# A two-layer attention and SwiGLU prompt on one core: next layer's first rounding in the middle of the last unit, layer 0's norms in two halves, the second chunk's transposes inside a product, input by two queues

## The chip, the cores and the metric

The kernel runs on one core of a Trainium2 chip. The metric is the device time of one execution in microseconds (us); for the kernel before it is the median of three runs. A profile comes from one further execution. The engines are TensorE (PE: matmuls and transposes; PEld: its weight loads), VectorE (DVE), ScalarE (ACT), GpSimd (POOL) and SyncE (SP, which here only issues DMAs). All instruction orders are written out by hand, so each engine executes its instructions in the order in which the program emits them, and waits in that order.

## The reference

The input `x` is 2048 rows of 448 floats. Two identical layers follow each other, each an attention with one key and value head for 16 query heads, and a SwiGLU feed-forward:

```python
# x: (1, 2048, 448); 16 heads of 28; wq (448, 448), wk, wv (448, 28), wo (448, 448)
def A(x):                                   # multi-query attention, no mask
    q = (x @ wq).reshape(1, 2048, 16, 28).transpose(0, 2, 1, 3)
    k, v = x @ wk, x @ wv
    p = softmax(einsum("bhqd,bkd->bhqk", q, k) * 28 ** -0.5)
    return einsum("bhqk,bkd->bhqd", p, v).transpose(0, 2, 1, 3).reshape(1, 2048, 448) @ wo
def B(x):                                   # w_gate, w_up (448, 1792); w_down (1792, 448)
    return (silu(x @ w_gate) * (x @ w_up)) @ w_down
for _ in range(2):                          # the same weights in both layers
    x = x + A(layernorm(x))                 # layernorm without gain and bias, eps 1e-5
    x = x + B(layernorm(x))
```

## The kernel before

The rows are cut into 16 tiles of 128 and four chunks (c = 0 to 3) of 512. `xres` holds all of `x` on the chip; every sum of a layer is added into it. Matmuls run on float32r operands: each operand is cut into a high part (a rounded copy, made by ScalarE or GpSimd) and a low part (value minus high part, made by VectorE or GpSimd), and a product is the sum of high times high, high times low and low times high. This cutting is called rounding below; `cut`, `flip` and `flipped` (L286 to L312) do it for a normed chunk: `xh` is the high part, `xl` the low one.

**The norm of a chunk** is made by `norm_steps` (L234). It returns a list of steps: four `stat` (two VectorE instructions each, L241 and L242, per tile of 128 rows), one `scale` (two GpSimd instructions, L246 and L247, which turn the four variances into `rstd`), and four `apply` (VectorE, L255: subtract the mean, multiply by `rstd`), each followed by a small copy on GpSimd (L257). With `away` given, the normed chunk is turned by VectorE and sent through DRAM (`send`, L265, `load`, L274); without it TensorE turns it (`flip`, L291: sixteen 128x128 transposes into four PSUM banks, four to a bank, L296), and ScalarE (`xh`, L304) and VectorE (`xl`, L309 and L312) round it from there.

**The projections** (`Attention.project`, L514) are sixteen products of 128 output columns, in the order of `self.order`: for each chunk the column blocks m = 3, 2, 0, 1. `self.seen` counts them from 0. One product (`product_T`, L318) is eleven matmuls of 128x128 by 128x512. Its result is copied out by ScalarE (L556, L558) and stored through DRAM; for m = 0 and 1 VectorE also transposes the value rows (`vt`, L565), after ScalarE's copy. Before the product whose successor (or which itself) is the first of a chunk, that chunk is flipped (`turned`); in layer 0 the flip of chunk 1 comes after product 3 instead of before it (`late`). `self.plan[n, 1]` and `self.when[n]` hold steps that are emitted after product n: there stand the norms of layer 0's chunks 1 to 3, the loads of the next chunk of `x` (`fill`), the key loads (`key_load`) and key splits (`key_split`, GpSimd).

**The scores** follow (`Attention.scores`), 256 steps per layer, and then **the feed-forward** (`FeedForward`): 14 blocks of 128 hidden columns in seven groups of two, the groups 2 to 5 by a block scheme of their own, the others as *units* (gi, c, n): group, chunk, block in the group. A unit (`unit`, L1069) is emitted in this order: eleven pairs of matmuls into two banks; `between`, one-column reads `seen` (L355) by ScalarE of both banks, which separate the two halves in which rows 0 to 63 and rows 64 to 127 write the same bank; the first of the two `down` steps of the unit before it, which ends with `between` on its four banks; ten more pairs into the same two banks; SiLU (L1110), product with the up half (L1111) and rounding of the result (`h`: L1112, `hl`: L1115), with the second `down` step among them; and then the entries of `self.soon` that are due. An entry of `soon` is a number and a function; each unit lowers the numbers of all entries in the order in which they were appended, and calls those that fall below zero. `self.mid[gi, c, n]` holds functions that a unit calls between its two halves: the first one ahead of the `down` step, the others behind it.

**The hand-over to layer 1.** In the last group (gi = 6), a chunk's last sums are added to `xres` in the first unit of the next chunk, and then `hand_over(c)` (L1035) is called: it emits the statistics and the scale of layer 1's norm of this chunk and appends what remains to `soon`. For chunk 0 that is two steps that apply, turn, send and load it; `cut` (L1053), which comes due in unit (6, 3, 0) and rounds it, four casts on ScalarE and four subtractions on VectorE; and the first three products of layer 1 (L1054), due in unit (6, 3, 1). For chunk 1 `ready` (L1044: the four applies) is appended in unit (6, 2, 0) and comes due in (6, 3, 0). After unit (6, 3, 1) follow the fourth product (with chunk 1's flip ahead of it) and `flush`, the last `down` steps.

**The start.** The four tiles of chunk 0 of `x` are loaded by SyncE (L1233), then the weights `wq`, `wk`, `wv` (`load_wqkv`) and chunk 1 (L1253). While these come, TensorE transposes the identity 54 times (L1252). The buffers that are filled with constants (`vsb`, `qraw`, `mask`, on GpSimd) come after chunk 0's norm.

Of the kernel before, what the change touches and what calls it, by code (L numbers as in the profile page):

```python
# [8 lines left out]
F32 = mybir.dt.float32  # L9
# [6 lines left out]
P = 128  # L16
# [36 lines left out]
def forward(  # L53
# [177 lines left out]
            again,  # L231
        )

    def norm_steps(c, away=None):  # L234


        got = {}
        cs = slice(4 * c, 4 * c + 4)

        def stat(t):  # L240
            nc.vector.bn_stats(stats[:, 4 * c + t, :], xres[:, 4 * c + t, :])  # L241
            nc.vector.bn_aggr(mv[:, 4 * c + t, :], stats[:, 4 * c + t, :])  # L242

        def scale():
            rstd = pers.tile([P, 4], F32, name="rstd", bufs=2)
            nc.gpsimd.tensor_scalar(rstd, mv[:, cs, 1], 1.0, EPS, ALU.mult, ALU.add)  # L246
            nc.gpsimd.tensor_tensor(rstd, rstd, halfn, ALU.pow)  # L247
            got["r"] = rstd

        def apply(t):  # L250
            if t == 0:
                got["x"] = pers.tile([P, 4, 512], F32, name="xn")
            got["o"] = (away() if away else got["x"][:, t, :])[:, 0:D]
            i, r = xres[:, 4 * c + t, :], got["r"][:, t : t + 1]
            nc.vector.tensor_scalar(got["o"], i, mv[:, 4 * c + t, 0:1], r, ALU.subtract, ALU.mult)  # L255
            if not away:
                nc.gpsimd.tensor_copy(got["x"][:, t, D:512], got["o"][:, 384:D])  # L257

        def turn(t):
            nc.vector.transpose(side()[:, :, :, t], got["o"].rearrange("p (k s) -> p k s", s=32))  # L260

        def side():
            return got["x"].rearrange("p t n -> p (t n)")[:, 0 : 4 * D].rearrange("p (k s t) -> p k s t", s=32, t=4)

        def send():  # L265
            turns.append(dram.tile([D, 512], F32, name=f"xt{len(turns)}"))
            got["xt"] = turns[-1]
            for a in range(4):
                nc.sync.dma_start(
                    got["xt"].rearrange("(k r) n -> r k n", r=32)[:, :, P * a : P * a + P],  # L270
                    side()[32 * a : 32 * a + 32].rearrange("p k s t -> p k (s t)"),
                )

        def load():  # L274
            got["raw"] = pers.tile([P, 4, 512], F32, name="xn")
            rows3(got["raw"], got["xt"])

        got["load"] = load
        fs = [lambda t=t: stat(t) for t in range(4)] + [scale]
        for t in range(4):  # L280
            fs += [lambda t=t: apply(t)] + [lambda t=t: turn(t)] * bool(away)
        return fs + [send] * bool(away), got
# [32 lines left out]

        return [(a[0][rs], b[0][rs]), (a[0][rs], b[1][rs]), (a[1][rs], b[0][rs])]

    def product_T(po, a_h, a_l, tiles, late=False):  # L318

        xh, xl = tiles[:2]  # L320
        seq, low = [], []
        for k in range(3):
            seq += [(a_h[k], xh[:, k, :]), (a_h[k], xl[:, k, :])]
            (low if late else seq).append((a_l[k], xh[:, k, :]))
        seq += low
        seq += [(a_h[3], xh[:, 3, :]), (a_l[3], xh[:, 3, :])]
        for i, (a, b) in enumerate(seq):
            nc.tensor.matmul(po, a, b, start=(i == 0), stop=(i == len(seq) - 1))  # L328

    def by_rows(upper, n, w, tiles):  # L330
# [28 lines left out]
    class Attention:  # L359
# [154 lines left out]
        def project(self):  # L514

            c, m = self.order[self.seen]
            for f in self.plan.get((self.seen, 0), ()):
                f()
            late = self.layer == 0 and self.seen == 3
            turned = [o[0] for o in self.order[self.seen : self.seen + 2] if o[1] == 3]  # L520
            for o in turned if not late else ():
                self.turned(o)
            self.q(c, m)
            for o in turned if late else ():
                self.turned(o)
            for f in self.plan.get((self.seen, 1), []) + self.when.pop(self.seen, []):
                f()
            self.seen += 1
# [2 lines left out]
            if c in self.norms:  # L531
                flip(self.norms.pop(c), self.X[c])

        def q(self, c, m):
            cs = slice(512 * c, 512 * c + 512)
            held, po = bank((3, 4, 5) if self.seen > len(self.order) - 4 else wide[-1], True)
            ms = slice(P * m, P * m + P)
            wh, wl = self.w
            product_T(po, [wh[:, k, ms] for k in range(4)], [wl[:, k, ms] for k in range(4)], self.X[c], self.layer + self.seen == 0)
            if not full and self.seen in (6, 10, 14):  # L540
                self.maxima(self.seen // 4 - 1)
            live.remove(held)
            if c not in self.qd:
                self.qd[c] = dram.tile([D, 512], F32, name=f"qd{self.layer}_{c}")
            last = self.seen == len(self.order) - 1
            raw = pers.tile([P, 512], F32, name="sg") if last else self.pool.tile([P, 512], F32, name="stage")
            if last:
                nc.scalar.copy(raw, po)
            if not full and (c or not self.layer):
                if self.seen % 2 == 0:  # L550
                    self.two = wpool.tile([P, 2, 512], F32R, tag="wgh", name="q2", bufs=FG + 1)
                self.hi[m] = self.two[0:112, self.seen % 2, :]
                if last:
                    self.rounded = lambda: nc.vector.tensor_copy(self.hi[m], raw[0:112, :])
                else:
                    nc.scalar.copy(self.hi[m], po[0:112, :])  # L556
            if not last:
                nc.scalar.copy(raw, po)  # L558
# [6 lines left out]
            nc.vector.transpose(vt, po[96:128, :])  # L565
# [217 lines left out]
    class FeedForward:  # L783
# [217 lines left out]
        def accumulate(self, gi, c, d):  # L1001
# [22 lines left out]
            def others():  # L1024
                for t in (2, 1, 3):
                    add(t)
                for t in (1, 3, 2):
                    store(t)
                live.difference_update(HIGH)
                if end and self.nxt:  # L1030
                    self.hand_over(c)

            return [begin, others]

        def hand_over(self, c):  # L1035

            a = self.nxt
            fs, got = norm_steps(c, None if c else lambda: qraw)
# [11 lines left out]
            if c == 0:  # L1050
                self.soon.append([1, lambda: [f() for f in fs[5:9]]])
                self.soon.append([2, lambda: [f() for f in (*fs[9:], got["load"], wipe)]])
                self.soon.append([4, lambda: cut(got, a.X[c])])  # L1053
                self.soon.append([5, lambda: [a.project() for _ in range(3)]])  # L1054
            elif c == 1:
                self.soon.append([2, ready])
            else:
                a.plan[4 * c - 4, 0] = [ready]

# [170 lines left out]
            self.flush()  # L1230

    for t in range(4):
        nc.sync.dma_start(xres[:, t, :], xs[:, t, :])  # L1233
    nc.gpsimd.memset(halfn, -0.5)
    nc.scalar.activation(warm, halfn[:, 0:1], AF.Exp)
    nc.gpsimd.memset(bottom, 0.0)
# [2 lines left out]
    at = Attention(0)  # L1239
    at.pool = xb.enter_context(tc.tile_pool(name="stage_", bufs=4))  # L1240
    xbp = xb.enter_context(tc.tile_pool(name="xb0", bufs=2))
    fs, got = norm_steps(0)
    for f in fs[:4]:
        f()
    parts, at.w = load_wqkv(xb.enter_context(tc.tile_pool(name="wqkv0", bufs=1)), True)
    make_identity(nc, ident)
    for f in fs[4:]:
        f()
    at.norms[0] = got
    idle = bank(LOW)[1]  # L1250
    for n in range(54):
        nc.tensor.transpose(idle[:, 0:P], ident, ident)  # L1252
    fill = lambda c: nc.sync.dma_start(xres[:, 4 * c : 4 * c + 4, :], xs[:, 4 * c : 4 * c + 4, :])  # L1253
    fill(1)
    at.below(nc.sync)
    at.X = {c: xtile(xpool if c < 2 else xbp) for c in range(NC)}
    parts[0]()
    at.turned(0)
    nc.gpsimd.memset(vsb, 0.0)
    nc.gpsimd.memset(vsb[:, :, DH : DH + 1], 1.0)  # L1260
    nc.gpsimd.memset(qraw, 0.0)
    if mask is not None:
        nc.gpsimd.memset(mask, 0.0)
        nc.gpsimd.memset(mask[:, 0:16:5, :], 1.0)
        for base, sign in ((0, 1), (DH - 1, -1)):
            nc.gpsimd.affine_select(
                out=mask, in_=mask, pattern=[[0, 16], [-DH * sign, 4]], compare_op=ALU.is_ge, fill=0.0,
                base=base, channel_multiplier=sign,
            )
    parts[1]()  # L1270
    for c in range(1, NC):
        fs, got = norm_steps(c)
        n = 4 * c - 4
        at.plan[n, 1] = [lambda c=c: fill(c + 1)] * (c < NC - 1) + fs[:5]
        at.plan[n + 1, 1] = fs[5:] + [lambda c=c, got=got: at.norms.__setitem__(c, got)]
    for layer in range(2):
        at.finish()
        xb.close()
# [33 lines left out]
```

## Time and profile before

| | before |
|---|---|
| three runs, us | 1967.7, 1967.4, 1964.23; median 1967.4 |
| the profiled execution's own time, us | 1967.23 |
| its span, first to last instruction, us | 1965.5 |
| mean granted clock of TensorE | 0.997 |
| busy: PE, PEld, DVE, ACT, POOL | 99%, 67%, 51%, 68%, 39% |
| products of layer 0 | about 12 to 63 us |
| scores of layer 0 | about 63 to 570 us |
| feed-forward of layer 0 | about 570 to 1000 us |
| layer 1 | about 1000 us to the end |

Rows of a timeline give the start, the duration, the engine, the line, the operation, output and inputs, the count where like ones were merged, and in brackets the idle time before it with what ended it. Rows of a table of windows give the stretch, its length, and the busy time (and instructions) of PE, PEld, DVE, ACT and POOL, then TensorE's granted clock (1.00 is full speed), the DMA engines' busy share and GB/s. Matmuls overlap in these rows: a dense row of them is read by the distance of the starts, not by the durations.

### The profile page before, as it was taken

How to read it: one execution, taken by the hardware profiler on the slowest of the kernel's cores; microseconds unless marked ns; L12 is line 12 of the kernel's file. 1: busy time of each engine (PE TensorE's matmuls, PEld its weight loads, DVE VectorE, ACT ScalarE, POOL GpSimd, SP SyncE). 2: the span in 40 equal slices, each digit the busy share in tenths (PEclk: the TensorE clock that was granted, in tenths of full speed). 3: DMA queues.
4: the chain of work that ended last, by engine and by line, in shares of the span. 5: the costliest groups of instructions: out<-in, count | busy, mean ns of one | idle time of the engine just before them, and what ended most of it. 6: DMA issues, size and time to landing. Idle time of an engine off the chain costs nothing. (4 is left out here: it accounts for less than half of the span.)

```text
span 1965.5 us, 45651 instructions
## 1 busy us (share of the span) xinstructions
PE 1950.6 (99%) x18315; PEld 1322.2 (67%) x18315; DVE 1012.1 (51%) x1711; ACT 1338.4 (68%) x2353; POOL 769.3 (39%) x989
## 2 busy tenths in 40 slices
PE   9999999999999999999999999999999999999998
PEld 7544545445458999999984445454454688999997
DVE  7443543544425566665654345435454346666653
ACT  4899797997963344444348997979979533444432
POOL 4212111122214868766332221111322157678640
PEclk9999999999999999999999999999999999999999
DMA  5101020121310110011131111102112101110102
GB/s 165 55 19 33 22 53 23 31 59 28 73 33 2 53 33 21 28 32 27 52 103 40 31 32 31 44 13 52 39 39 61 33 4 51 33 32 21 28 17 77
DMA packets 100001, 79.69 MB, mean 41 GB/s; under 512 B 26024, under 2 KB 82984, under 8 KB 99784
## 3 DMA queue, kind: packets, MB, share of 16 engines
q1 hardware_dynamic: 99496, 76.27, 14.5%
q8 instruction: 144, 2.36, 0.5%
q14 instruction: 73, 0.60, 0.1%
q10 hardware_dynamic: 288, 0.46, 0.1%
HBM read 57.15 MB, written 18.74 MB: 39 GB/s over the span
## 5 line engine op out<-in xcount | busy, mean ns | idle before, releaser
L672 PE MATMUL bank<-pt,vsb 128*32 128x512 f32 x4096 | 493.3, 598 | 0.3
L631 PE MATMUL bank<-qstack,keys 32*128 32x512 f32 x1536 | 484.6, 425 | 0.0
L631 PE MATMUL three<-qstack,keys 32*128 32x512 f32 x4608 | 460.7, 425 | 1.5 <-DVE vt L565 1.2
L631 PEld LDWEIGHTS three<-qstack,keys 32*128 32x128 f32 x4608 | 254.6, 182 | 295.0 <-ACT pt L644 178.6
L638 ACT ACTIVATE pt<-three 128x1536 f32<-128x1536 f32 x256 | 372.1, 1453 | 1.2 <-PE bank L672 0.8
L644 ACT ACTIVATE pt<-three 128x1536 f32<-128x1536 f32 x256 | 371.7, 1452 | 0.0
L348 PE MATMUL bank<-xh,wgh 64*128 64x512 f32 x1344 | 360.5, 393 | 3.8 <-ACT seen L355 3.5
L348 PE MATMUL bank<-wdh,h 64*128 64x448 f32 x1776 | 327.0, 364 | 0.1
L640 DVE COPY raw<-bank 128x512 f32<-128x512 f32 x256 | 177.3, 693 | 226.6 <-PE bank L631 224.4
L348 PE MATMUL bank<-xh,wgl 64*128 64x512 f32 x1020 | 289.7, 391 | 0.0
L682 DVE TENSOR_TENSOR o<-bank,o 128x512 f32<-128x512 f32 x224 | 154.9, 691 | 240.3 <-PE bank L672 235.3
L672 PEld LDWEIGHTS bank<-pt,vsb 128*32 128x32 f32 x4096 | 107.1, 109 | 249.6 <-issue 153.3
L711 POOL TENSOR_TENSOR o<-o 128x512 f32<-128x512 f32 x32 | 41.2, 1286 | 591.7 <-DMA o<-rd 423.4
L355 ACT COPY seen<-bank 128x1 f32<-128x1 f32 x788 | 99.1, 163 | 240.9 <-PE bank L348 180.8
L348 PE MATMUL bank<-xl,wgh 64*128 64x512 f32 x912 | 251.9, 391 | 0.0
L631 PEld LDWEIGHTS bank<-qstack,keys 32*128 32x128 f32 x1536 | 243.4, 183 | 1.2 <-DVE o L682 0.6
L348 PEld LDWEIGHTS bank<-wdh,h 64*128 64x128 f32 x1776 | 231.6, 184 | 8.9 <-issue 2.0
L348 PE MATMUL bank<-wdl,h 64*128 64x448 f32 x888 | 208.2, 366 | 0.0
L348 PEld LDWEIGHTS bank<-xh,wgh 64*128 64x128 f32 x1344 | 196.1, 185 | 16.1 <-ACT seen L355 3.9
L897 POOL TENSOR_TENSOR xres<-stage,xres 128x448 f32<-128x448 f32 x120 | 151.5, 1274 | 113.2 <-ACT stage L890 113.2
L862 DVE TENSOR_TENSOR xn<-bank,xn 128x512 f32<-128x512 f32 x192 | 126.5, 687 | 127.2 <-PE bank L348 94.3
L643 ACT ACTIVATE pt<-bank 128x512 f32<-128x512 f32 x256 | 151.0, 590 | 59.7 <-PE bank L631 59.5
(202 smaller groups left out, 3069.1 us busy)
## 6 DMA issues: line engine op xcount, KB each, us to landing
o<-rd SPq DMA_DIRECT2D x32, 256.0 KB
qraw<-qd SPq DMA_DIRECT2D x128, 56.0 KB
qd<-stage SPq DMA_DIRECT2D x30, 224.0 KB
xt<-xn SPq DMA_DIRECT2D x28, 224.0 KB
wdr<-in_B_w_down_dram SPq DMA_DIRECT2D x28, 224.0 KB
wr<-in_B_w_gate_dram SPq DMA_DIRECT2D x32, 192.0 KB
wr<-in_B_w_up_dram SPq DMA_DIRECT2D x32, 192.0 KB
xn<-xt SPq DMA_DIRECT2D x7, 768.0 KB
```

Of the source, the lines that this page charges most:

```text
L348: nc.tensor.matmul(po, a, b, start=start, stop=stop, skip_group_check=True)
L355: nc.scalar.copy(seen[:, i : i + 1], po[:, 0:1])
L631: nc.tensor.matmul(three[:, j, :] if j < 3 else one, k[js, kp, ks], q[js, part, :], start=(z == 0), stop=(z == 2), tile_position=(32 * j, 0),)
L638: nc.scalar.activation(pt, three, AF.Exp, scale=SCALE)
L640: nc.vector.tensor_copy(raw, one)
L643: nc.scalar.activation(pt1, one, AF.Exp, scale=SCALE)
L644: nc.scalar.activation(pt, three, AF.Exp, scale=SCALE)
L672: nc.tensor.matmul(po[32 * j : 32 * j + 32, :], vsb[:, n % NT, :], pts[n][j], start=(n == 2 * d), stop=(n > 2 * d), skip_group_check=True,)
L682: nc.vector.tensor_tensor(acc, in_turn(po), acc, ALU.add)
L711: nc.gpsimd.tensor_tensor(rb, oraw, rb, ALU.mult)
L862: plus = lambda out, po, r: tt(by_tile(out), in_turn(po), by_tile(r), ALU.add)
L897: nc.gpsimd.tensor_tensor(r, h[e, t], r, ALU.add)
```

## The change

Five things are changed. (1) `hand_over` takes the group number, and the rounding of layer 1's chunk 0 no longer stands in `soon` but in `self.mid[6, 3, 1]`, behind the `down` step in the middle of that unit; `ready` of chunk 1 comes due one unit later. (2) `norm_steps` takes `n`; with `n = 2`, as for layer 0's attention, `scale` is made for two tiles at a time, first 0 and 1, then 2 and 3. All `stat` steps still come first. (3) Layer 0's flip of chunk 1 is emitted inside product 3, ahead of its eighth matmul. (4) Chunk 0 of `x` is loaded by SyncE and ScalarE in turn. (5) The constants are filled before chunk 0's scale, there are 46 warm-up transposes instead of 54, and the norm of layer 0's chunk 3 is planned one product earlier (after products 7 and 8 instead of 8 and 9). The loads of chunks 2 and 3 keep their places.

```diff
-    def norm_steps(c, away=None):
+    def norm_steps(c, away=None, n=1):
...
-        def scale():
-            rstd = pers.tile([P, 4], F32, name="rstd", bufs=2)
-            nc.gpsimd.tensor_scalar(rstd, mv[:, cs, 1], 1.0, EPS, ALU.mult, ALU.add)
-            nc.gpsimd.tensor_tensor(rstd, rstd, halfn, ALU.pow)
-            got["r"] = rstd
+        def scale(z):
+            m = 4 // n
+            rstd = pers.tile([P, 4], F32, name="rstd", bufs=2)[:, 0:m]
+            nc.gpsimd.tensor_scalar(rstd, mv[:, 4 * c + m * z : 4 * c + m * z + m, 1], 1.0, EPS, ALU.mult, ALU.add)
+            nc.gpsimd.tensor_tensor(rstd, rstd, halfn[:, 0:m], ALU.pow)
+            got["r"] = got.get("r", []) + [rstd[:, t : t + 1] for t in range(m)]
...
-        fs = [lambda t=t: stat(t) for t in range(4)] + [scale]
+        fs = [lambda t=t: stat(t) for t in range(4)] + [lambda z=z: scale(z) for z in range(n)]
...
-    def product_T(po, a_h, a_l, tiles, late=False):
+    def product_T(po, a_h, a_l, tiles, late=False, amid=()):
...
         for i, (a, b) in enumerate(seq):
+            for f in amid if i == 7 else ():
+                f()
             nc.tensor.matmul(po, a, b, start=(i == 0), stop=(i == len(seq) - 1))
...
-            self.q(c, m)
-            for o in turned if late else ():
-                self.turned(o)
+            self.q(c, m, [lambda o=o: self.turned(o) for o in turned] if late else [])
...
-        def hand_over(self, c):
+        def hand_over(self, gi, c):
...
-                self.soon.append([4, lambda: cut(got, a.X[c])])
+                self.mid[gi, 3, 1] = [lambda: None, lambda: cut(got, a.X[c])]
                 self.soon.append([5, lambda: [a.project() for _ in range(3)]])
             elif c == 1:
-                self.soon.append([2, ready])
+                self.soon.append([3, ready])
...
-        nc.sync.dma_start(xres[:, t, :], xs[:, t, :])
+        (nc.scalar if t % 2 else nc.sync).dma_start(xres[:, t, :], xs[:, t, :])
...
-    fs, got = norm_steps(0)
+    fs, got = norm_steps(0, n=2)
...
-    for f in fs[4:]:
-        f()
-    at.norms[0] = got
-    idle = bank(LOW)[1]
-    for n in range(54):
...
     nc.gpsimd.memset(qraw, 0.0)
...
+    for f in fs[4:]:
+        f()
+    at.norms[0] = got
+    idle = bank(LOW)[1]
+    for n in range(46):
...
     for c in range(1, NC):
-        fs, got = norm_steps(c)
-        n = 4 * c - 4
-        at.plan[n, 1] = [lambda c=c: fill(c + 1)] * (c < NC - 1) + fs[:5]
-        at.plan[n + 1, 1] = fs[5:] + [lambda c=c, got=got: at.norms.__setitem__(c, got)]
+        fs, got = norm_steps(c, n=2)
+        n = 4 * c - 4 - (c == 3)
+        at.plan[n, 1] = fs[:6]
+        at.plan[n + 1, 1] = fs[6:] + [lambda c=c, got=got: at.norms.__setitem__(c, got)]
+        if c > 1:
+            at.plan[4 * c - 8, 1].insert(0, lambda c=c: fill(c))
```

More of the change, by code (lines that the diff above doesn't have):

```diff
@@ L232, in xtile @@
         )
-    def norm_steps(c, away=None):
+    def norm_steps(c, away=None, n=1):
         got = {}
-        cs = slice(4 * c, 4 * c + 4)
         def stat(t):
@@ L253, in apply @@
             got["o"] = (away() if away else got["x"][:, t, :])[:, 0:D]
-            i, r = xres[:, 4 * c + t, :], got["r"][:, t : t + 1]
+            i, r = xres[:, 4 * c + t, :], got["r"][t]
             nc.vector.tensor_scalar(got["o"], i, mv[:, 4 * c + t, 0:1], r, ALU.subtract, ALU.mult)
@@ L532, in turned, with q @@
                 flip(self.norms.pop(c), self.X[c])
-        def q(self, c, m):
+        def q(self, c, m, amid=()):
             cs = slice(512 * c, 512 * c + 512)
@@ L538, in q @@
             wh, wl = self.w
-            product_T(po, [wh[:, k, ms] for k in range(4)], [wl[:, k, ms] for k in range(4)], self.X[c], self.layer + self.seen == 0)
+            product_T(po, [wh[:, k, ms] for k in range(4)], [wl[:, k, ms] for k in range(4)], self.X[c], self.layer + self.seen == 0, amid)
             if not full and self.seen in (6, 10, 14):
@@ L1030, in others @@
                 if end and self.nxt:
-                    self.hand_over(c)
+                    self.hand_over(gi, c)
             return [begin, others]
-        def hand_over(self, c):
+        def hand_over(self, gi, c):
             a = self.nxt
@@ L1246, in forward @@
     make_identity(nc, ident)
-    for f in fs[4:]:
-        f()
-    at.norms[0] = got
-    idle = bank(LOW)[1]
-    for n in range(54):
[L1252 to L1258, printed above, removed]
     nc.gpsimd.memset(vsb, 0.0)
@@ L1269, in forward @@
             )
+    for f in fs[4:]:
[3 more added lines that the diff above has]
+    for n in range(46):
+        nc.tensor.transpose(idle[:, 0:P], ident, ident)
+    fill = lambda c: nc.sync.dma_start(xres[:, 4 * c : 4 * c + 4, :], xs[:, 4 * c : 4 * c + 4, :])
+    fill(1)
+    at.below(nc.sync)
+    at.X = {c: xtile(xpool if c < 2 else xbp) for c in range(NC)}
+    parts[0]()
+    at.turned(0)
     parts[1]()
     for c in range(1, NC):
-        fs, got = norm_steps(c)
-        n = 4 * c - 4
-        at.plan[n, 1] = [lambda c=c: fill(c + 1)] * (c < NC - 1) + fs[:5]
-        at.plan[n + 1, 1] = fs[5:] + [lambda c=c, got=got: at.norms.__setitem__(c, got)]
+        fs, got = norm_steps(c, n=2)
[4 more added lines that the diff above has]
+            at.plan[4 * c - 8, 1].insert(0, lambda c=c: fill(c))
     for layer in range(2):
```

## The prediction

> **What bounds the kernel now.** I read the page's engine shares first, then who TensorE waited for, then the timelines of TensorE, ScalarE, VectorE and GpSimd around the two places that the diff touches.
>
> ```profile
> span 1965.5 us, 45651 instructions
> PE 1950.6 (99%) x18315; PEld 1322.2 (67%) x18315; DVE 1012.1 (51%) x1711; ACT 1338.4 (68%) x2353; POOL 769.3 (39%) x989
> ...
> PE bank L348 <- ACT seen L355: 3.5, 1, 3.5
> ```
>
> TensorE is marked busy 99% of the span, so only small holes are left; its longest wait for another engine is one of 3.5 us, on ScalarE's one-column read `seen` (L355). The timelines show it in the last unit of layer 0's feed-forward, (6, 3, 1):
>
> ```profile
> 954.65 0.53 PE L348 MATMUL bank<-xh,wgh 64*128 64x512 f32 x2
> 956.95 0.51 PE L348 MATMUL bank<-wdh,h 64*128 64x448 f32 x2
> 958.18 0.53 PE L348 MATMUL bank<-xh,wgh 64*128 64x512 f32 x2
> ...
> 976.41 0.40 PE L348 MATMUL bank<-wdh,h 64*128 64x448 f32 x2
> 980.29 0.79 PE L348 MATMUL bank<-xh,wgh 64*128 64x512 f32 x2 [3.47 <-ACT seen L355]
> 986.63 0.50 PE L328 MATMUL bank<-xh,wh 128*128 128x512 f32 x1
> ...
> 977.94 2.18 ACT L304 CAST xh<-xn 128x512 fp32r<-128x512 f32 x4 [3.24 <-DMA xn<-xt]
> 980.03 0.53 ACT L355 COPY seen<-bank 128x1 f32<-128x1 f32 x6
> ...
> 980.52 0.69 DVE L312 TENSOR_TENSOR xh<-xn,xh 64x512 fp32r<-64x512 f32 x1
> 981.24 1.79 DVE L255 TENSOR_SCALAR xn<-xres,mv,rstd 128x448 f32<-128x448 f32 x4
> ```
>
> The rounding of layer 1's chunk 0 (four casts, L304) stands in ScalarE's queue ahead of the six `seen` reads. It waits until 977.94 for the load of `xn`; the reads come at 980.03, and TensorE may not overwrite the banks before them. The clock suffers too:
>
> ```profile
> 975.75:979.16 3.41, 1.06 (x11) 0.68 (x8) 2.74 (x8) 1.22 (x3) 1.91 (x3) 1.00 0.64 193
> 979.16:982.58 3.42, 2.29 (x10) 1.81 (x12) 3.35 (x8) 1.40 (x8) 0.96 (x3) 0.50 0.02 5
> 982.58:985.99 3.41, 3.41 (x20) 2.77 (x18) 0.85 (x3) 0.60 (x1) 0.75 (x3) 0.50 0.00 0
> 985.99:989.40 3.41, 3.41 (x20) 2.62 (x17) 0.99 (x2) 0.62 (x1) 0.00 (x0) 1.00 0.00 0
> ```
>
> The column after POOL's is the granted clock. After a stretch of 3.41 us in which TensorE worked 1.06 us it is halved for 6.83 us; the second of these stretches, busy from its first moment, is still at half.
>
> **Part 1: the rounding moved into the middle of (6, 3, 1).** At full clock the upper ten pairs of a unit take 2.30 us (954.65 to 956.95) and the second half of `down` 1.23 us (956.95 to 958.18). Without the wait they start at about 976.6, one step of 0.2 us after 976.41, so the first product of layer 1 starts at 976.6 + 2.30 + 1.23 = 980.2 instead of 986.63. That removes 6.4 us: 3.5 of wait and 2.9 of half clock. The casts keep their time, since the load is not touched. They now stand ahead of this unit's SiLU: it starts when they end, at 980.1, a microsecond after its products. That costs nothing, for `hl` is then done by about 983.5 and nobody reads it before the flush behind four products of 2.5 us each. VectorE's subtractions end at 981.2 as before; the first product, started at 980.2, reaches the last chunk two microseconds in. No stall there.
>
> **Part 2: chunk 1's norm comes one unit later, and this adds a wait.** `ready` for chunk 1 (its four applies L255, at 981.24 before) fired in unit (6, 3, 0). With 3 in place of 2 it fires in (6, 3, 1), in the same sweep of `soon` as the three products, and behind them, since their entry was appended earlier. So VectorE's queue holds the third product's transpose (L565) ahead of the applies, and TensorE's next work, the transposes of chunk 1 ahead of the fourth product, needs all four applies.
>
> ```profile
> 994.02 0.39 PE L328 MATMUL bank<-xh,wl 128*128 128x512 f32 x1
> 994.25 1.47 PE L296 MATMUL bank<-ident,xn 128*128 128x128 f32 x12
> 996.61 0.50 PE L328 MATMUL bank<-xh,wh 128*128 128x512 f32 x1
> ...
> 995.11 0.72 DVE L565 STREAM_TRANSPOSE vt<-bank 32x512 f32<-32x512 f32 x1 [7.45 <-ACT stage L558]
> ...
> 22.87 1.91 PE L296 MATMUL bank<-ident,xn 128*128 128x128 f32 x16
> 24.69 0.50 PE L328 MATMUL bank<-xh,wh 128*128 128x512 f32 x1
> ```
>
> Count from M, the start of the third product's last matmul (994.02 here). L565 ends at M+1.81, four applies of 0.45 end at M+3.64, the last transpose of the first group goes at M+3.7, and twelve more at 0.114 each (16 from 22.87 to 24.69) end at M+5.2. Before, the fourth product started at M+2.59. So 2.6 us of new wait, with TensorE nearly still from M+0.2 to M+3.7: 3.5 us with three transposes in it, about as long as the hole that was removed. Queued behind the applies on VectorE are chunk 1's own subtractions, needed only by the fifth product.
>
> Does this hole halve the clock again? The stretches have no fixed place in the kernel. A 3.5 us hole leaves one aligned stretch of 3.41 us with at most 1.06 us of work, which is known to halve it, in (2 x 1.06 + 0.1) / 3.41, say two cases in three; in the rest the fuller stretch still idles half its time. The cost runs from nothing to 3.4 us (6.83 us at half); one stretch at half is 1.7, and the row of the old hole says 2.9. I take 2.3, between the last two. Part 1 and 2 together: -6.4 + 2.6 + 2.3 = -1.5 us, with ends -3.8 and -0.4.
>
> On this the Trainium skill's page "TensorE: Matmul & The Clock Gate" (Part 1: The HAM clock gate) says that half rate comes after at least one idle window of about 3.4 us. Taken strictly the new hole, with transposes in it, would never halve the clock, and parts 1 and 2 would give -3.8; the row of 975.75 differs, since 1.06 us of work stood in that stretch. It is a rival below.
>
> **Part 3: the start.**
>
> ```profile
> 1.89 8.28 PE L1252 MATMUL bank<-ident 128*128 128x128 f32 x54 [1.89 <-POOL ident masks.py:199]
> 2.00:4.00 2.00, 2.00 (x10) 2.00 (x11) 0.61 (x1) 0.36 (x2) 0.00 (x0) 1.00 0.95 293
> ...
> 6.13 0.63 DVE L241 BATCH_NORM_STATS2 stats<-xres 128x6 f32<-128x448 f32 x1 [1.17 <-DMA xres<-in_A_x_dram]
> 6.79 0.18 DVE L242 BATCH_NORM_AGGREGATE mv<-stats 128x2 f32<-128x6 f32 x1
> 6.89 0.59 DVE L241 BATCH_NORM_STATS2 stats<-xres 128x6 f32<-128x448 f32 x1
> 7.52 0.18 DVE L242 BATCH_NORM_AGGREGATE mv<-stats 128x2 f32<-128x6 f32 x1
> 9.14 1.78 DVE L255 TENSOR_SCALAR xn<-xres,mv,rstd 128x448 f32<-128x448 f32 x4 [1.44 <-POOL rstd L247]
> ```
>
> Statistics end at 7.70, GpSimd's two steps hold the applies for 1.44 us, the applies end at 10.92, and everything up to the first product follows from them. In two halves the first `rstd` is ready while tiles 2 and 3 are still measured, so two applies (0.89) go inside the 1.44 us, and the last ends at 7.70 + 1.44 + 0.89 = 10.03: 0.9 us earlier. The shorter warm-up (46 of 54 transposes; the last eight at 0.114) ends at about 9.3, ahead of that. The memsets that moved ahead on GpSimd run while it waits for the statistics. For the two queues I take nothing: the DMA share is already 0.95 from 2 to 4 us. Ends: if the last tile came earlier by two issue times the gain grows by 0.9; if tile 2 landed only with tile 3, since the two now share the engines, the statistics end 0.76 later and 0.1 is left.
>
> Chunk 1's transposes inside product 3:
>
> ```profile
> 20.38 0.39 PE L328 MATMUL bank<-xh,wh 128*128 128x512 f32 x1
> 21.96 0.39 PE L328 MATMUL bank<-xl,wh 128*128 128x512 f32 x1
> 28.16 0.39 PE L328 MATMUL bank<-xh,wh 128*128 128x512 f32 x1
> ...
> 20.29 1.78 DVE L255 TENSOR_SCALAR xn<-xres,mv,rstd 128x448 f32<-128x448 f32 x4 [1.42 <-POOL rstd L247]
> ```
>
> A product of eleven at 0.226 (20.38 to 21.96 is seven) takes 2.5 us; the one from 24.69 took until 28.16, 1.0 us more, because its `xl` came off VectorE too late. With the transposes before the eighth matmul (at 21.96), four matmuls cover the rounding, and 1.0 us goes. They find their data: by halves the applies end at 21.2 instead of 22.1. If they did not, the wait would merely move there.
>
> Chunk 3 measured one product earlier:
>
> ```profile
> 42.95 0.62 POOL L139 TENSOR_SCALAR keys<-wrk 128x512 fp32r<-128x512 f32 x1
> 45.04 0.20 POOL L246 TENSOR_SCALAR rstd<-mv 128x4 f32<-128x4 f32 x1
> 46.37 1.78 DVE L255 TENSOR_SCALAR xn<-xres,mv,rstd 128x448 f32<-128x448 f32 x4 [2.32 <-POOL rstd L247]
> 46.95 2.89 PE L296 MATMUL bank<-ident,xn 128*128 128x128 f32 x16
> 49.60 0.48 PE L328 MATMUL bank<-xh,wh 128*128 128x512 f32 x1
> ```
>
> Sixteen transposes took 46.95 to 49.60 instead of 1.8 us: 0.8 us lost, because `rstd` stood behind the key split on GpSimd. Now `rstd` stands ahead of it; the halves go at 42.95 and 44.25, the applies end at 46.4 instead of 48.15, and up to 0.8 us goes. The key split ends 2.6 us later, and with it SyncE's next key load and the stores behind it; four stage buffers cover that, and its keys are read by the scores only. If GpSimd's chain, which starts from a load, did not move up with the products, the three gains would meet at this point and leave 1.7 in place of 2.7.
>
> Sum of the start: 0.9 + 1.0 + 0.8 = 2.7 us, ends 1.0 and 3.6. **All parts: 2.7 + 1.5 = 4.2 us** off the profiled execution's own 1967.2, which stands 0.2 below the median of 1967.4: 1963.0.
>
> **Rivals.** (1) The new hole does not halve the clock: 1967.2 - 2.7 - 3.8 = 1960.7. For it: three transposes lie in the hole, and a split over two stretches leaves each half busy. Against: 1.06 us of work did not help before. Chance 0.2. (2) The hand-over's gain is eaten (two full stretches at half, 3.4 us: -0.4) or the start keeps only 1.0 of its 2.7 us: 1964.1 to 1966. Speaking for it: the new hole is as long as the old. Chance 0.2. (3) Slower: the tiles of `x` on the second queue share the engines with the weights, which SyncE now issues two DMAs earlier, and the warm-up ends at 9.3. If the last apply then came after about 11.7 (the last tile some 1.7 us later than 6.89), the hole behind the warm-up would be the 2.4 us that a halved stretch had, and the products would start at half clock: 0.7 + 3.4, against 1.0 + 0.8 + 1.5 kept: 1968, and a microsecond more for each that the tile is later still. Against it: SyncE issues tile 2 before any weight. Chance 0.05, counted as slower altogether. (4) The order in the `soon` list is not what I read and `ready` comes ahead of L565: no new hole, 1967.2 - 2.7 - 6.4 = 1958. Chance 0.05.
>
> **How the numbers follow.** The forecast has 0.5. The three runs before spread over 3.5 us, about 0.2%, which is what a measurement of this kernel can tell; faster by more than that means under 1963.5. The forecast's case falls on both sides (0.28 below, 0.22 above), rivals 1 and 4 below, rival 2 inside: faster 0.53, same 0.42, slower 0.05. The range, 1959.5 to 1966.7, takes in rivals 1 and 2 with about a microsecond of spread.
>
> **What would show it.** In the profile of the changed kernel TensorE's 3.5 us wait on `seen` L355 is gone and the casts L304 stand behind the six reads; in its place TensorE's transposes (L296) wait some 3 us on VectorE's L255 behind L565 at about 990, with or without a granted clock of 0.5 there. The last apply of chunk 0 ends near 10.0, the product after chunk 1's transposes takes 2.5 us, chunk 3's transposes 1.8. The prediction is wrong if the applies precede L565, if the first statistics wait longer for `x`, or if the last product of the start gains less than 1.5 us on its old time.

## The result and the profile after

| | before | after |
|---|---|---|
| runs | 19 | 19 |
| median, us | 1967.27 | 1963.13 |
| lowest to highest, us | 1964.23 to 1968.62 | 1961.34 to 1965.06 |
| profiled execution's own time, us | 1967.23 | 1962.70 |
| its span, us; mean granted clock | 1965.5; 0.997 | 1960.9; 1.000 |

The change is worth 4.1 us: the ratio of the times is 0.998, with a 95% interval of 0.9973 to 0.9987. The forecast was 1963.0, a gain of 4.2.

The page after, and who TensorE waited for (us in total, times, longest):

```profile
span 1960.9 us, 45644 instructions
PE 1947.1 (99%) x18307; PEld 1319.9 (67%) x18307; DVE 1016.9 (52%) x1711; ACT 1339.3 (68%) x2353; POOL 771.3 (39%) x997
...
PE bank L296 <- DVE xn L255: 2.1, 1, 2.1
PE bank L1263 <- POOL ident masks.py:199: 1.9, 1, 1.9
PE three L631 <- DVE vt L565: 1.2, 2, 0.6
PE three L614 <- POOL onl L140: 0.7, 1, 0.7
```

The 3.5 us wait on `seen` is gone; the transposes' wait on `xn` has come in its place. (Line numbers move by up to 11: products are now at L330, feed-forward matmuls at L350, `seen` at L357.) The timelines of TensorE, ScalarE and VectorE at the hand-over:

```profile
976.71 0.39 PE L350 MATMUL bank<-wdh,h 64*128 64x448 f32 x2
977.02 0.49 PE L330 MATMUL bank<-xh,wh 128*128 128x512 f32 x1
...
984.42 0.39 PE L330 MATMUL bank<-xh,wl 128*128 128x512 f32 x1
986.90 2.91 PE L296 MATMUL bank<-ident,xn 128*128 128x128 f32 x16 [2.09 <-DVE xn L255]
989.90 0.50 PE L330 MATMUL bank<-xh,wh 128*128 128x512 f32 x1
...
973.63 0.29 ACT L357 COPY seen<-bank 128x1 f32<-128x1 f32 x3 [0.45 <-PE bank L350]
974.70 2.19 ACT L304 CAST xh<-xn 128x512 fp32r<-128x512 f32 x4 [0.79 <-DMA xn<-xt]
...
985.51 0.72 DVE L565 STREAM_TRANSPOSE vt<-bank 32x512 f32<-32x512 f32 x1 [5.44 <-ACT stage L558]
986.27 1.85 DVE L255 TENSOR_SCALAR xn<-xres,mv,rstd 128x448 f32<-128x448 f32 x4
```

The casts stand behind the reads and TensorE passes from the unit to the products without a gap. The applies stand behind the third product's L565, and TensorE starts no matmul between 984.42 and 986.90. The first product of layer 1 starts at 977.02 instead of 986.63, the fourth at 989.90 instead of 996.61.

The start, TensorE's and VectorE's timelines:

```profile
4.34 0.63 DVE L240 BATCH_NORM_STATS2 stats<-xres 128x6 f32<-128x448 f32 x1 [4.34 <-DMA xres<-in_A_x_dram]
...
7.18 0.18 DVE L241 BATCH_NORM_AGGREGATE mv<-stats 128x2 f32<-128x6 f32 x1
7.28 0.90 DVE L255 TENSOR_SCALAR xn<-xres,mv,rstd 128x448 f32<-128x448 f32 x2
8.78 0.99 DVE L255 TENSOR_SCALAR xn<-xres,mv,rstd 128x448 f32<-128x448 f32 x2 [0.59 <-POOL rstd L247]
...
20.86 1.91 PE L296 MATMUL bank<-ident,xn 128*128 128x128 f32 x16
22.53 0.48 PE L330 MATMUL bank<-xl,wh 128*128 128x512 f32 x1
23.54 0.40 PE L330 MATMUL bank<-xh,wh 128*128 128x512 f32 x1
26.04 0.39 PE L330 MATMUL bank<-xh,wh 128*128 128x512 f32 x1
...
44.66 2.17 PE L296 MATMUL bank<-ident,xn 128*128 128x128 f32 x16
46.58 0.48 PE L330 MATMUL bank<-xh,wh 128*128 128x512 f32 x1
...
60.22 0.51 PE L631 MATMUL three<-qstack,keys 32*128 32x512 f32 x3
```

Chunk 0's last apply ends at 9.77 instead of 10.92. The product behind chunk 1's transposes runs from 23.54 to 26.04, 2.5 us where it took 3.5. Chunk 3's transposes take 1.92 us (44.66 to 46.58) where they took 2.65. The scores start at 60.22 where they started at 63.25.

### The profile page after: what moved, and what is told of

Same layout as the page of the kernel before. It is cut to its first block, busy times and chain, and to the rows that moved or that the text cites. A ratio compares the mean times of both kernels' runs of the same rounds, so it can differ in the third digit from the quotient of the medians.

```text
span 1960.9 us, 45644 instructions
## 1 busy us (share of the span) xinstructions
PE 1947.1 (99%) x18307; PEld 1319.9 (67%) x18307; DVE 1016.9 (52%) x1711; ACT 1339.3 (68%) x2353; POOL 771.3 (39%) x997
## 5 line engine op out<-in xcount | busy, mean ns | idle before, releaser
L350 PE MATMUL bank<-xh,wgh 64*128 64x512 f32 x1344 | 364.5, 392 | 0.3 <-DVE sg L1111 0.3
L350 PE MATMUL bank<-wdh,h 64*128 64x448 f32 x1776 | 329.4, 364 | 0.1
L350 PE MATMUL bank<-xh,wgl 64*128 64x512 f32 x1020 | 291.8, 390 | 0.0
L357 ACT COPY seen<-bank 128x1 f32<-128x1 f32 x788 | 100.2, 163 | 243.4 <-PE bank L350 182.4
L350 PE MATMUL bank<-xl,wgh 64*128 64x512 f32 x912 | 254.9, 390 | 0.0
L350 PEld LDWEIGHTS bank<-wdh,h 64*128 64x128 f32 x1776 | 237.7, 184 | 9.5 <-issue 2.0
L350 PE MATMUL bank<-wdl,h 64*128 64x448 f32 x888 | 213.2, 366 | 0.0
L350 PEld LDWEIGHTS bank<-xh,wgh 64*128 64x128 f32 x1344 | 200.3, 184 | 11.6 <-DVE sg L1111 0.7
```

What stands on the lines that cost most here:

```text
L350: nc.tensor.matmul(po, a, b, start=start, stop=stop, skip_group_check=True)
L357: nc.scalar.copy(seen[:, i : i + 1], po[:, 0:1])
```

## The experiments

Margins below are the kernel's median less that of the kernel before in the same comparison (1966.48, 1966.19 and 1966.64 us). The first four kernels shared one comparison, the next four another, the last stood alone.

**The hand-over alone**, on the kernel before:

```diff
-                    self.hand_over(c)
+                    self.hand_over(gi, c)
...
-                self.soon.append([4, lambda: cut(got, a.X[c])])
+                self.mid[gi, 3, 1] = [lambda: None, lambda: cut(got, a.X[c])]
...
-                self.soon.append([2, ready])
+                self.soon.append([3, ready])
```

> The kernel before with only the hand-over changed (rounding of layer 1's chunk 0 in the middle of unit (6, 3, 1), ready of chunk 1 one unit later). Theory: the 3.5 us wait on the one-column reads goes and the first product of layer 1 starts 6.4 us earlier, 980.2 in place of 986.6 in the profile; the transposes of chunk 1 then wait for the four applies, and the fourth product gives 2.9 us back; with the clock halved in most runs by the new hole as by the old one, the time is 1 to 3 us under that of before, about 1965.5. Rival: the whole gain of the change comes from the start, and this part alone gives 0 (1967.3), because the new hole costs as much as the old one.

1964.39 us in 11 runs, ratio 0.9989 (0.998 to 0.9998): a margin of -2.1, inside the 1 to 3 us that were expected. In its profile the new hole halves the clock, which it did not in the profile of after. TensorE's timeline, and the table of windows:

```profile
980.25 0.49 PE L328 MATMUL bank<-xh,wh 128*128 128x512 f32 x1
...
987.65 0.39 PE L328 MATMUL bank<-xh,wl 128*128 128x512 f32 x1
990.13 4.30 PE L296 MATMUL bank<-ident,xn 128*128 128x128 f32 x16 [2.09 <-DVE xn L255]
994.09 0.61 PE L328 MATMUL bank<-xh,wh 128*128 128x512 f32 x1
```

```profile
987.80:991.20 3.40, 1.12 (x5) 0.46 (x3) 2.42 (x5) 0.59 (x1) 1.42 (x5) 0.97 0.28 84
991.20:994.60 3.40, 3.40 (x16) 3.16 (x16) 1.89 (x4) 1.89 (x4) 0.77 (x4) 0.53 0.00 0
994.60:998.00 3.40, 3.40 (x21) 2.64 (x21) 1.33 (x3) 1.21 (x3) 0.00 (x0) 1.00 0.00 0
```

One stretch at half, not two: the fourth product starts 13.84 us after the first, against 12.88 in after, so the halving cost 0.96 us here; it begins, at about 991.0, while the transposes still wait for the applies, which end at 991.35. How often the hole halves the clock is not shown: this profile's mean clock, 0.998, is that of two of the eleven runs, and the 0.999 of the other nine leaves it open, since the profile of the start alone, below, has 0.999 with one halved stretch.

**The start alone**: the kernel after with the two lines of the hand-over put back.

```diff
-                self.mid[gi, 3, 1] = [lambda: None, lambda: cut(got, a.X[c])]
+                self.soon.append([4, lambda: cut(got, a.X[c])])
...
-                self.soon.append([3, ready])
+                self.soon.append([2, ready])
```

> The changed kernel with the hand-over put back (the rounding in unit (6, 3, 0), ready of chunk 1 there too). Theory: the scores of layer 0 start at 60.2 as in the changed kernel, 3.0 us earlier than before, all of this stays to the end, and the 3.5 us wait with the half clock behind it is there again: 1964.3. Rival: the start is given back later (the scores have their own bound), and the time is that of before, 1967.3.

1964.40 us in 11 runs, ratio 0.999 (0.9981 to 0.9999): -2.1, where 3.0 was expected; the interval, -0.2 to -3.7, holds both. The two halves add up to the whole, -4.2 against -4.1, each with some 1.8 us of interval to either side. In its profile the old hole is there again and halves the clock for one stretch (977.9 to 981.3), not for two. TensorE's timeline:

```profile
977.57 0.56 PE L350 MATMUL bank<-xh,wgh 64*128 64x512 f32 x2 [3.56 <-ACT seen L357]
...
982.88 0.50 PE L330 MATMUL bank<-xh,wh 128*128 128x512 f32 x1
```

From the upper pairs to the first product it takes 5.31 us, 1.8 more than the 3.53 at full clock; in the profile of the kernel before it took 6.34 (980.29 to 986.63), 2.8 more.

**The applies ahead of L565**: the same change, but `ready` is put first in the list, so it is emitted ahead of the three products.

```diff
-                self.soon.append([3, ready])
+                self.soon.insert(0, [3, ready])
```

> The changed kernel with one difference: ready of chunk 1 is put at the head of the list of due entries, so that its four applies stand in VectorE's queue ahead of the third product's transpose, not behind it. Theory: they run right behind the rounding of h at about 980 to 982, the transposes of chunk 1 at 984.6 find them done, the fourth product starts 2.9 us earlier, no hole over 1 us is left in the hand-over, and the mean clock is 0.999 or more in every run: 1963.1 - 2.9 - about 1 for the clock = 1959.2. Rival 1: the clock costs nothing, because what it loses was hidden: 1960.2. Rival 2: the gain is lost again in the scores of layer 1, 1963.

1958.91 us in 5 runs, from 1958.60 to 1959.39, ratio 0.9961 (0.9947 to 0.9974): -7.6. This beats both kernels. The timelines of VectorE and TensorE:

```profile
980.48 1.78 DVE L255 TENSOR_SCALAR xn<-xres,mv,rstd 128x448 f32<-128x448 f32 x4
985.84 0.72 DVE L565 STREAM_TRANSPOSE vt<-bank 32x512 f32<-32x512 f32 x1 [3.58 <-ACT stage L558]
...
977.34 0.49 PE L330 MATMUL bank<-xh,wh 128*128 128x512 f32 x1
...
984.97 1.47 PE L296 MATMUL bank<-ident,xn 128*128 128x128 f32 x12
986.70 0.63 PE L296 MATMUL bank<-ident,xn 128*128 128x128 f32 x4 [0.26 <-DVE vt L565]
987.33 0.50 PE L330 MATMUL bank<-xh,wh 128*128 128x512 f32 x1
```

The applies run at 980.48, the transposes find their data, and the fourth product starts 9.99 us after the first, as before the change (9.98). So the hole comes from the order of the list alone, and costs about 3.4 us of median (7.57 less 4.14, from two comparisons). The slowest of these five runs, 1959.39, is below the fastest of after, 1961.34.

**One queue for the input**, on the kernel after:

```diff
-        (nc.scalar if t % 2 else nc.sync).dma_start(xres[:, t, :], xs[:, t, :])
+        nc.sync.dma_start(xres[:, t, :], xs[:, t, :])
```

> The changed kernel with all four tiles of the input loaded by SyncE again. Theory: in the changed kernel tile 0 came 0.95 us later than before, but tiles 1 to 3 so early that VectorE never waited for them, and the statistics ended at 7.36 in place of 7.70; by one queue they end at 7.7 again and the last apply at 10.1 in place of 9.8: 0.3 us slower, 1963.5, not to be told from no change in the times but in the profile. Rival: the second queue is what made the start faster by more than the halves, 0.9 us slower without it: 1964.0.

1962.78 us in 11 runs, ratio 0.998 (0.9971 to 0.9989): -3.7. That is 0.4 behind after's -4.1, as expected, and not to be told from no difference. The profile shows the statistics end later:

```profile
7.33 0.63 DVE L240 BATCH_NORM_STATS2 stats<-xres 128x6 f32<-128x448 f32 x1 [0.46 <-DMA xres<-in_A_x_dram]
8.00 0.18 DVE L241 BATCH_NORM_AGGREGATE mv<-stats 128x2 f32<-128x6 f32 x1
```

at 8.18 instead of 7.36. In this execution the transposes of chunk 3 also wait 1.04 us for their applies, and the scores start only at 62.23; the one-queue kernel further down shows no such wait. The same edit was made on the better kernel, whose times spread less, together with three that each take one part of the start away. **No halves for chunk 0**:

```diff
-    fs, got = norm_steps(0, n=2)
+    fs, got = norm_steps(0)
```

> The kernel with the applies first (1958.9, five runs within 0.8 us, so that a term of half a microsecond can be seen), with chunk 0's norm of layer 0 in one piece again. Theory: the last apply of chunk 0 ends 0.8 us later (statistics' end + 1.44 + four applies of 0.45, in place of + 1.42 + two), and with it the scores start 0.8 us later: 1959.7. Rival: the rounding behind it waits for something else, the weights or TensorE's warm-up, and the scores start as before: 1958.9.

**The transposes of chunk 1 behind product 3:**

```diff
-            self.q(c, m, [lambda o=o: self.turned(o) for o in turned] if late else [])
+            self.q(c, m)
+            for o in turned if late else ():
+                self.turned(o)
```

> The kernel with the applies first, with layer 0's transposes of chunk 1 behind product 3 again. Theory: product 4 waits 1.0 us for its low parts as in the kernel before, and all of it stays: 1959.9. Rival: chunk 3's stall, whose release hangs on a load and not on the products, absorbs it: 1958.9, with chunk 3's transposes 1 us denser.

**Chunk 3's norm at its old place:**

```diff
-        n = 4 * c - 4 - (c == 3)
+        n = 4 * c - 4
```

> The kernel with the applies first, with the norm of layer 0's chunk 3 after products 8 and 9 again. Theory: its scale steps stand behind the key split (1.9 us) on GpSimd, the transposes of chunk 3 wait for the applies, 1.3 to 1.9 us in all instead of 0.4: 1959.9 to 1960.4. Rival: by halves the norm is early enough on its own, and nothing changes: 1958.9.

**One queue again:**

```diff
-        (nc.scalar if t % 2 else nc.sync).dma_start(xres[:, t, :], xs[:, t, :])
+        nc.sync.dma_start(xres[:, t, :], xs[:, t, :])
```

> The kernel with the applies first, with the input by SyncE alone. The changed kernel with one queue showed the statistics' end at 8.18 in place of 7.36 to 7.57, and the kernels before 7.70 and 8.20. Theory: the second queue is worth what the issue times of two DMAs are, 0.6 us on the last tile: 1959.5. Rival 1: 0 (1958.9), as the times of that kernel, 1962.8, let it seem. Rival 2: chunk 3's stall grows with it as in that kernel's profile (1.0 us): 1960.5.

| kernel | runs | median (lowest to highest), us | ratio (95%) | scores start, us |
|---|---|---|---|---|
| applies first | 5 | 1958.91 (1958.60 to 1959.39) | 0.9961 (0.9947 to 0.9974) | 60.55 |
| one queue | 5 | 1958.83 (1957.56 to 1959.55) | 0.9961 (0.9947 to 0.9974) | 60.92 |
| no halves | 6 | 1959.88 (1959.10 to 1961.27) | 0.9967 (0.9955 to 0.9979) | 61.56 |
| flip behind product 3 | 5 | 1959.86 (1959.00 to 1960.01) | 0.9965 (0.9951 to 0.9978) | 61.62 |
| chunk 3 later | 5 | 1959.96 (1959.12 to 1963.22) | 0.9965 (0.9952 to 0.9978) | 64.12 |

For the three parts the time of the theory came, for the one queue that of its rival 1: the second queue is worth nothing that the times show. Each of the three parts is worth about 1.0 us of median, counted from the one-queue kernel of the same comparison; the intervals overlap, so it is the profiles that carry the size. Without halves all four applies wait on one `rstd` and end at 10.84 (VectorE's timeline):

```profile
9.06 1.78 DVE L255 TENSOR_SCALAR xn<-xres,mv,rstd 128x448 f32<-128x448 f32 x4 [1.44 <-POOL rstd L247]
```

With the flip behind product 3, TensorE's timeline shows the product after it take 3.48 us (23.66 to 27.14), waiting for `xl`:

```profile
23.66 0.49 PE L330 MATMUL bank<-xh,wh 128*128 128x512 f32 x1
24.65 0.50 PE L330 MATMUL bank<-xl,wh 128*128 128x512 f32 x1 [0.50 <-DVE xl L309]
...
27.14 0.40 PE L330 MATMUL bank<-xh,wh 128*128 128x512 f32 x1
```

With chunk 3 later, the profiled execution was the slowest of its kernel, 1963.22 us, 3.3 above the median; the other four lie at 1959.12 to 1960.55. The stall on `xn` halved the clock there. That accounts for about 1.6 us: the fourteen transposes from 47.08 take 3.11 us to the next product (50.19), where thirteen take 1.39 in the kernel with the applies first (45.52 to 46.91). The rest is not accounted for. TensorE's timeline and the windows:

```profile
45.91 0.75 PE L296 MATMUL bank<-ident,xn 128*128 128x128 f32 x2 [1.10 <-DVE xn L255]
47.08 3.46 PE L296 MATMUL bank<-ident,xn 128*128 128x128 f32 x14 [0.42 <-DVE xn L255]
```

```profile
43.98:47.39 3.41, 1.79 (x7) 0.76 (x5) 1.88 (x4) 0.99 (x2) 2.77 (x8) 1.00 0.45 138
45.00:46.00 1.00, 0.09 (x1) 0.10 (x1) 0.66 (x2) 0.00 (x0) 0.83 (x3) 1.00 0.16 51
46.00:47.00 1.00, 0.56 (x2) 0.18 (x2) 0.83 (x3) 0.00 (x0) 0.77 (x3) 1.00 0.59 180
47.00:48.00 1.00, 0.83 (x4) 0.64 (x5) 0.97 (x3) 0.00 (x0) 0.66 (x2) 0.69 0.25 55
48.00:49.00 1.00, 1.00 (x6) 1.00 (x5) 0.93 (x3) 0.72 (x2) 0.00 (x0) 0.50 0.26 102
```

**The hole filled**, on the kernel after: TensorE transposes the identity 18 times, into a bank nobody reads, while it waits. If the halved clock is what makes the hole cost more than its wait, this brings that part back and no more.

```diff
             turned = [o[0] for o in self.order[self.seen : self.seen + 2] if o[1] == 3]
+            if self.layer and self.seen == 3:
+                idle = bank(wide[-1])[1]
+                for _ in range(18):
+                    nc.tensor.transpose(idle[:, 0:P], ident, ident)
```

> The changed kernel with 18 transposes of the identity into a free bank ahead of chunk 1's transposes in layer 1 (some 2.05 us of work for TensorE inside the hole in which it waits for the applies; nothing reads them). The wait for the applies stays as it is. Theory: the hole costs 2.9 us by its length alone, and a half clock only in some of the runs; filled, the clock is never halved there, every run has a mean clock of 0.999 or more, the fourth product starts 12.9 us behind the first as in the changed kernel's profile, and the time is that of its runs at clock 1.000, 1962.5, some 4.5 under before. Rival 1: the clock is what makes the times of this kernel spread over 3.7 us; then they now lie within 1 us, as those of the kernel with the applies first do. Rival 2: transposes of the identity don't count as work, the clock is halved as often as before, and the time stays at 1963.1.

1961.66 us in 11 runs, from 1960.52 to 1962.92, ratio 0.9975 (0.9966 to 0.9984): -5.0, where some -4.5 was expected. That is 0.8 more than after's -4.1, but the two intervals overlap. The fourth product is not earlier, 990.14, 12.88 us after the first, exactly as in after; every run has a mean granted clock of 0.999 or 1.000, where 12 of after's 19 had 0.998. Six of these eleven had 1.000, against two of the 41 runs of the kernels with the hole open (after, the hand-over alone, one queue). Rival 1 did not come: the times spread over 2.4 us, not 1, so the clock in this hole is not all that spreads those of after (3.7). TensorE's timeline:

```profile
984.89 2.13 PE L526 MATMUL bank<-ident 128*128 128x128 f32 x18
987.23 2.82 PE L296 MATMUL bank<-ident,xn 128*128 128x128 f32 x16 [0.21 <-DVE xn L255]
990.14 0.50 PE L330 MATMUL bank<-xh,wh 128*128 128x512 f32 x1
```

## Why the prediction was right, and where its terms were off

**Part 1, -6.4.** The start of the first product was put at 980.2 (its sum gives 980.13); with the hand-over alone it is 980.25. In this one execution the term holds. In the medians it is smaller: applies-first and start-alone differ only by the hand-over without its hole, and stand 5.5 us apart (1964.40 less 1958.91). The prediction took both its parts from one profile in which the old hole halved the clock for two stretches, at a mean clock of 0.997. Of the 27 runs of the kernel before beside the first four experiments, six had that clock (mean 1967.56 us); the other 21 lay at 0.998 to 1.000, about 1.3 us lower. The profile of the start alone shows the hole with one halved stretch: 3.6 us of wait and 1.8 of clock, close to the 5.5. So the likeliest reading is that the wait was right and the clock's part, 2.9, was one draw, on the high side; its median was not measured by itself.

**Part 2, 2.6 of wait and 2.3 of clock.** The wait has the place and the cause named. It costs 2.9 us (12.88 less 9.98 between the first and the fourth product): L565 ends 1.81 us after M as worked out and the applies at M + 3.70 (worked out: 3.64), but from there to the product it takes 1.8 us instead of 1.6. The clock term was mis-sized. The step that failed is its price of 2.3, put between one stretch (1.7) and the old hole (2.9), as if all the work under the halved clock were late by it, and charged in full. Here the halved stretch begins while the transposes still wait for the applies, and the fourth product was late by 0.96 in the hand-over alone and by 0.95 in the profile of one queue (986.84 to 993.27, 6.43 us from M, against 5.48 in after). And only a part of the runs pay it: the profiled execution of after paid nothing, its 12 runs at 0.998 were 0.8 us slower in the mean than its other seven (1963.54 against 1962.72), and the filled hole returned 0.8 of median. The working itself had given the halving two cases in three, but the sum took it as certain. The whole hole costs 3.4, not 4.9. The errors of parts 1 and 2 came from the same profiled execution and in part cancel: -5.5 + 3.4 = -2.1, where the text had -6.4 + 4.9 = -1.5. That sum is after less the start alone; the runs of the hand-over alone, measured apart, have -2.1 too (-0.4 to -3.9).

This bears on the rule of the Trainium skill's page "TensorE: Matmul & The Clock Gate" (Part 1: The HAM clock gate), by which half rate comes after at least one idle window. The runs contradict the strict reading: the clock was halved behind 3.40 us with 1.12 us of work in them (the row 987.80 of the hand-over alone), and in the chunk-3 kernel behind 3.41 us with 1.79 (the row 43.98). Nor is it certain that such a hole halves it, since the same hole in the profile of after left it alone:

```profile
984.40:987.80 3.40, 1.12 (x5) 0.33 (x3) 2.25 (x5) 0.59 (x1) 1.30 (x4) 1.00 0.33 101
987.80:991.20 3.40, 3.22 (x20) 2.57 (x21) 2.33 (x5) 2.06 (x4) 0.89 (x4) 1.00 0.00 0
```

Rival 1, no halving, thus describes some executions of after, its profiled one among them: at the fourth product this one stands 6.7 us ahead of before, where rival 1 had 6.5.

**Part 3, 2.7.** The profile gives 3.0 (scores at 60.22 against 63.25): 1.15 at chunk 0 (0.9 worked out), 1.0 at chunk 1, 0.7 at chunk 3, 0.2 at chunk 2, on which the prediction said nothing. Over the profiles it is 2.5 to 3.0: the scores start at 60.22 to 60.58 in the four with the whole new start (after, start alone, applies first, hole filled) and at 63.25 and 63.08 in the two with the old one. The term for chunk 3 is the least settled: in the hand-over alone, with that norm as it was before, the transposes take 1.97 us (47.48 to 49.45), where they took 2.65 before. Taking the second queue as nothing was off in the profiles: the statistics end at 7.36 to 7.62 in the seven with it and at 7.70 to 8.20 in the four without it. In times nothing of it is seen. The runs of the start alone say 2.1, with an interval from 0.2 to 3.7 (0.9999 to 0.9981 of 1966.48), so 2.7 and 3.0 both fit.

**The sum.** -2.1 and -2.1 give the 4.2 of the forecast, which had them as -1.5 and -2.7. That the total was met to 0.1 us is in part luck: a hand-over larger and a start smaller in the medians than worked out make up for each other, within intervals wider than either error. The profiled execution, 1962.70, came near 1963.0 by yet another way: it has no halved clock in the hole, and loses about as much later. It is 6.7 us ahead at the fourth product of layer 1, but only 4.9 ahead at layer 1's feed-forward (its first SiLU at 1542.62 against 1547.54). Some 1.8 us went in layer 1's scores, where the output projection (L614) waited 1.0 us on GpSimd's rounding (the row `onl L140` and one of 0.3 on `onh L139`). The two profiles with the old start (before, hand-over alone) have no such wait, the other eight with the new one from none to 0.7 us. Its cause was not tried and stays open.

Rival 4, `ready` ahead of L565, did not happen, but its mechanism was right: with `ready` put there the hole is gone. Its time, 1958, was met (1958.91) partly because the kernel before was 0.8 us faster in that comparison: the margin is -7.6, where the working had -9.1, too much by the same clock and start terms. Rival 3, a slower start because the tiles come late, had its first step: the first tile does come later with two queues (first statistics at 4.34 instead of 3.39). But the last came earlier, and the last one sets the applies.

## What to carry to other kernels

When work is moved to a later point of a hand-written order, look at what stands ahead of it on its engine there: a list swept in the order of appending put four applies behind a transpose that had to wait for the third product, and one `insert(0, ...)` was worth nearly as much as the whole change (3.4 against 4.1 us). A clock term read from one profile is one draw: price it from many runs, multiply it by the chance that it is paid, and ask whether the work under the halved clock waits for another engine anyway (0.96 us here against 1.8 where it did not). Where a hole can't be closed, idle transposes in it kept the clock up here; the 0.8 us of median that they brought lie within overlapping intervals. Small gains ahead of a shared path are best seen by taking them away one at a time, in a kernel whose times spread little (0.8 us here).

## What the runs showed of the hardware

- Transposes of the identity kept the clock up: with 18 of them in the hole all 11 runs had a mean clock of 0.999 or more and six had 1.000, against two of 41 with the hole open. The Trainium skill's page "TensorE: Matmul & The Clock Gate" (Part 4: PE-mode transpose) says that transposes do not count as busy in the same way for the clock; these float32 ones of 128x128 did count. (The rows name them MATMUL, so whether they ran in the mode that the page means is not shown.)
- Short waits can halve the clock: in the chunk-3 kernel it fell at about 47.4, after 1.10 and 0.42 us of waiting with two transposes between; the 3.41 us up to there hold 1.79 us of work (the row 43.98), more than half.
- Half rate lasted one stretch of 3.4 us in the four profiles in which TensorE was busy nearly all through that stretch (3.41 us of work in the hand-over alone, 3.41 in the start alone, 3.42 with one queue, 3.32 in the chunk-3 kernel), and two in the kernel before, where it worked 2.29 us in the first and 3.41 in the second. That the first stretch was not full is the likely reason; it was not tried.
- Two queues for four equal loads changed when the tiles came: in seven profiles with two queues the first tile's statistics start at 4.34 to 4.59, the four tiles are measured without a gap, and the statistics end at 7.36 to 7.62; in four with one queue they start at 3.39 to 3.56, wait 0.9 to 1.5 us for the third tile, and end at 7.70 to 8.20.
